# A block of r, k and w with 128 rows instead of 112

## The chip, the cores and the metric

The kernel runs on one core of one Trainium2 chip. The time is that of the device, in microseconds, from one launch; the median of several runs is given. A profile is one further execution, recorded by the hardware profiler; its span runs from the first instruction to the last, and its own time is a little longer.

The names of the engines in the profile: PE is TensorE (PEld its weight loads), DVE is VectorE, ACT is ScalarE, POOL is GpSimd, SP is SyncE, which issues nearly all transfers here.

## The reference

A linear attention with a decaying state (RWKV6) over 4 x 8 heads, 768 steps and 48 columns a head, then a feed-forward block with a hard-swish gate over the 3072 tokens (384 columns, 2048 inside).

```python
for t in range(S):
    kt, vt, rt, wt = (k[:, :, t], v[:, :, t], r[:, :, t], w[:, :, t])
    cur = np.einsum('bhd,bhe->bhde', u[None] * kt, vt)
    y[:, :, t] = np.einsum('bhd,bhde->bhe', rt, state + cur)
    state = wt[:, :, :, None] * state + np.einsum('bhd,bhe->bhde', kt, vt)
...
h = x @ w_in
relu6 = np.clip(h + 3.0, 0.0, 6.0)
g = h * relu6 / 6.0
return (g @ w_out).astype(np.float32)
```

The attention's inputs are 32-bit floats. The weights w_in and w_out come as 64-bit floats, which the kernel converts by itself.

## The kernel before

The sequence is cut into chunks of 128 steps: 4 sequences of 6 chunks, 24 chunks in all (NT). Four chunks make a block of 512 tokens, of which there are 6, and the feed-forward part works block by block. The program for all engines is one list of named steps. Each step has an engine, a function that issues its instructions, and the steps that it must follow; the order of the list is written out by hand in a table (ORDER). Each engine works through its own steps in that order.

For a chunk i, the host lays r, k and w out in DRAM as one block, `feat[i]`. Its rows are the columns of the heads: 48 for the even heads, 16 unused ones, 48 for the odd heads, together GP + D = 64 + 48 = 112. Each row holds 1545 floats, or 6180 bytes: r (512), k (512), and w in 8 pieces of 65 with a final word. On the chip the block lands in a tile `feat_in` of a pool with three buffers. The step feat{i} (load_feat, L343) loads it. The first chunk is loaded in two parts: the columns of w first, and r and k by load_rest (L353). The three buffers also serve the steps refetch{k}, which from about 150 us on read w and the weight words once more, 128 rows of 6144 bytes each, to test their range.

What reads a block, by line:

- L428 (DVE): a scan backwards over w, giving E; L437 (DVE): a scan forwards, giving W
- L448 and L452 (DVE for the first seven chunks, POOL after that): k times E, giving K, and r times W, over W
- L461 (DVE): rk, r times k, for the first nine chunks; PE multiplies it with u (L473) to get the diagonal. For later chunks POOL computes rk from another load, rk_in (L366, then L464)
- PE turns K (L514) and multiplies K with W (L498) for the scores, and so on to the output x of the attention

The weight words come in 16 blocks (step fetch{j}, L391, tile `bits`). ACT makes `more` from them (L400, L405), DVE makes `top` (L411) and adds the two to `w_in` or `w_out` (L415). The feed-forward matmuls stand at L714 and L733 for the first block of tokens, and at L829 and L884 for the others. The latter use sums of weights and inputs that DVE forms beforehand (L776 and the lines after it). L846 and L854 (DVE) and L850 (ACT) belong to the gate, and L902 (DVE) to the output.

In the first 60 us the program has filler matmuls (L1260, on an identity matrix) on PE, put between the steps while the program is built, from a table of assumed times.

SP's queue begins like this (name of the tile, source, rows x elements); bits are the weight words, v_in the values v:

```order
1 L346 DMA feat_in<-in_feat_dram 112x521
2 L354 DMA feat_in<-in_feat_dram 112x1024
3 L349 DMA feat_in<-in_feat_dram 112x1545
4 L361 DMA v_in<-in_tok_dram 128x384
5 L391 DMA bits<-in_moe_w_in_dram 128x3x256
6 L361 DMA v_in<-in_tok_dram 128x384
7 L391 DMA bits<-in_moe_w_in_dram 128x3x256 x2
8 L349 DMA feat_in<-in_feat_dram 112x1545
```

The first two rows are the first chunk's block, the third and the eighth are the next two blocks.

The function general_path holds a second, slower way for inputs out of range. It is behind a branch that these inputs do not take, and the change touches its loads only so that they read the same 112 rows as before.

Of the kernel before, what the change touches and what calls it, by code (L numbers as in the profile page):

```python
# [8 lines left out]
F32 = mybir.dt.float32  # L9
# [12 lines left out]
HL = L // 2  # L22
GP = 64
# [220 lines left out]
def fast_path(tc, feat, tok, wflat, ub, ug, moe_w_in, moe_w_out, out, flag, n_chunks):  # L244
# [3 lines left out]


    nc = tc.nc  # L250
    NT, PR, nf = feat.shape
    HD = tok.shape[3]
    D = PR - GP
    H = HD // D
    P = H // 2
# [11 lines left out]
    with ExitStack() as ctx:  # L267
        const = ctx.enter_context(tc.tile_pool(name="const", bufs=1))
        io = ctx.enter_context(tc.tile_pool(name="io", bufs=3))
# [6 lines left out]
        chunk_of = [(i // NSEQ * 2 + i % 2) * n_chunks + i % NSEQ // 2 for i in range(NT)]  # L276
# [8 lines left out]
        st = [dict() for _ in range(NT)]  # L285
# [52 lines left out]
        n = P * L  # L338
# [2 lines left out]
        plan.ring("rk_in", 2)  # L341

        def load_feat(i):  # L343
            a = io.tile([PR, nf], F32, name="feat_in")
            if i == 0:
                nc.sync.dma_start(out=a[:, 2 * n:], in_=feat[chunk_of[i], :, 2 * n:])  # L346
                nc.scalar.dma_start(out=u_col, in_=ug)
            else:
                nc.sync.dma_start(out=a, in_=feat[chunk_of[i]])  # L349
            st[i].update(a=a, r=a[:, :n].rearrange("q (x t) -> q x t", t=HL),  # L350
                         k=a[:, n:2 * n].rearrange("q (x t) -> q x t", t=HL), w=a[:, 2 * n:])

        def load_rest():  # L353
            nc.sync.dma_start(out=st[0]["a"][:, :2 * n], in_=feat[chunk_of[0], :, :2 * n])  # L354

        def load_u():
            nc.sync.dma_start(out=u_bc, in_=ub.to_broadcast([128, HD]))
# [612 lines left out]
        def when(i):  # L970

            bk, c = divmod(i, BC)
            return BASE[bk] - LAG - (BASE[bk] - BASE[bk - 1]) / BC * (BC - 1 - c) if bk else -99.0
# [20 lines left out]
        for i in range(NT):  # L994
            t = when(i)
            k = START[i] if i < len(START) else when(i - 2) - AHEAD
            first, last = is_first(i), is_last(i)
            dve = i < EARLY
            behind = [f"fetch{BEHIND[i]}"] if i < len(BEHIND) and BEHIND[i] >= 0 else []
            plan.add(f"feat{i}", "SP", 0.45 if i else 1.15, do(load_feat, i), behind + [f"feat{i - 1}"] * (i > 0) + ["later"] * (i == 1), k - 20, kb=735 if i else 294,  # L1000
                     hold=[("feat", [f"K{i}", f"R{i}"] + [f"own{i}"] * (i < BY_PE))])
            plan.add(f"tok{i}", "SP", 0.45, do(load_tok, i), behind + [f"feat{i}"] * (i > 1) + ["later"] * (i < 2), k - 19.9, kb=320,
# [25 lines left out]
            t = k + 1 if i < len(START) else t  # L1028
# [25 lines left out]
            bk, c = divmod(i, BC)  # L1054
# [34 lines left out]

        plan.add("u", "SP", 0.45, load_u, ["fetch3"], -60.0, kb=320)  # L1090
        plan.add("later", "SP", 0.45, load_rest, ["feat0"], key=-999.0, kb=630)

        for j in range(len(pairs)):
            t = CONV[0] + j * CONV[1]
# [12 lines left out]
        for f in range(NFC):  # L1107
            for c0, c1 in parts_of[f]:
                m, x = c1 - c0, c0 // BY_SUM
# [47 lines left out]
        for bk in range(NB):  # L1157
# [7 lines left out]
            for d in range(2 * (bk > 0)):  # L1165
                at = K + U_ / 2 * d
                u, r = f"up{bk}.{d}.", f"read{bk}.{d}."
                name = lambda x: u + str(x) if isinstance(x, int) else r + x
# [41 lines left out]
            for p in range(2 * (bk > 0)):  # L1210
# [4 lines left out]
                d_, r, g_ = f"down{bk}.{p}.", f"out{bk}.{p}.", f"sum{bk}.{p}."  # L1215
# [26 lines left out]
        for k, (which, j) in enumerate(vets):  # L1242
            i = 8 + k // 2
# [23 lines left out]
def general_path(tc, feat, tok, ug, moe_w_in, moe_w_out, out, n_chunks):  # L1267
# [7 lines left out]


    nc = tc.nc
    NT, PR, nf = feat.shape
    HD = tok.shape[3]
    D = PR - GP  # L1280
    H = HD // D
    P = H // 2
# [4 lines left out]
    n2 = 2 * P * L  # L1287

    with ExitStack() as ctx:
        const = ctx.enter_context(tc.tile_pool(name="g_const", bufs=1))  # L1290
        io = ctx.enter_context(tc.tile_pool(name="g_io", bufs=3))
# [4 lines left out]
        st = [dict() for _ in range(NT)]  # L1296

        def load(i):
            a = io.tile([PR, 3, P, L], F32, name="rkw_in")
            b = io.tile([L, H, D], F32, name="v_in", bufs=4)  # L1300
            nc.sync.dma_start(out=a[:, 0:2].rearrange("q c p t -> q (c p t)"), in_=feat[i, :, :n2])
            nc.sync.dma_start(out=a[:, 2].rearrange("q p (a t) -> q (p a) t", a=2),
                              in_=feat[i, :, n2:nf - 1].rearrange("q (x t) -> q x t", x=2 * P)[:, :, 1:])
            nc.sync.dma_start(out=b.rearrange("s h d -> s (h d)"), in_=tok[i, :, 2, :])
            st[i].update(R=a[:, 0], K=a[:, 1], tot=a[:, 2], v=b)

        load(0)
        ub_sb = const.tile([PR, P, 2], F32, name="ub_sb")
        nc.sync.dma_start(out=ub_sb, in_=ug)
        load(1)  # L1310

        w_in = const.tile([128, NFC, NCC, 128], F32, name="w_in_g")
# [24 lines left out]
        for i in range(NA):  # L1337
            a = const.tile([128, 2, P, L], F32, name=f"scores_{i}")
# [147 lines left out]
        for i in range(NT):  # L1486
            if i + 2 < NT:
                load(i + 2)
            own(i)
            for l in range(LEVELS):  # L1490
                score(i, l)
                merge(i, l)
            read(i)
            write(i)
            turn(i)
            if i % GBC == GBC - 1:
                for f in range(NFC):
                    up(i // GBC, f)
                for c in range(GBC):
                    down(i // GBC, c)  # L1500
# [3 lines left out]
def kernel(  # L1504
# [25 lines left out]
    flags = ctx.enter_context(tc.tile_pool(name="flags", bufs=1))  # L1530
    flag = flags.tile([1, 1], I32, name="flag")
    fast_path(tc, feat, tok, wflat, ub, ug, moe_w_in, moe_w_out, out, flag, n_chunks)
    bad = nc.values_load(flag[0:1, 0:1], min_val=0, max_val=128)
    with tc.If(bad > 0):
        general_path(tc, feat, tok, ug, moe_w_in, moe_w_out, out, n_chunks)
# [64 lines left out]
```

## Time and profile before

| | |
|---|---|
| median of 3 runs | 546.07 us (544.54 to 546.16) |
| profiled execution | 545.16 us, span 543.4 us |
| PE busy | 533.5 us, 98% of the span |
| DVE, ACT, POOL busy | 78%, 49%, 20% |
| transfers of queue 1 (SP) | 63.12 MB, 38.0% of the DMA engines' time |
| loads of a block | 24, of 675.9 KB each, median 5.6 us to landing |

A row of the waits reads: engine and step that waited, what ended the wait, then microseconds in total, times, and the longest. A row of the timeline reads: start, length, engine, line, operation, output and inputs, shapes, and in brackets the idle time just before it with what ended it. A row of the transfers gives the number, the size of each and the median time from issue to landing. A row of a stretch gives its length and, for each engine, busy time and instructions, then PE's clock, the mean busy share of the 16 DMA engines, and GB/s.

### The profile page before, as it was taken

The page shows a single profiled execution, that of the slowest core. Times are in us where ns is not written, and L with a number is a line of the kernel's source. Part 1 is how long each engine was busy: PE and PEld are TensorE (multiplying, and loading weights), DVE is VectorE, ACT ScalarE, POOL GpSimd, SP SyncE. Part 2 cuts the span into 40 slices and gives each one's busy share as a digit, 9 for nine tenths or more (in the row PEclk, how much of TensorE's full clock was granted, in tenths as well). Part 3 has the DMA queues.
Part 4 walks back from the last instruction along what each step waited for, and adds up shares of the span by engine and source line. Part 5 has one row for each costly group of instructions (what it writes and reads, how often), then busy time and mean ns, then how long its engine had stood idle before and what let it go on. Part 6 is the DMA issues. An engine that isn't in the chain of part 4 may idle for free.

```text
span 543.4 us, 13407 instructions
## 1 busy us (share of the span) xinstructions
PE 533.5 (98%) x5558; PEld 468.2 (86%) x5558; DVE 423.5 (78%) x726; ACT 267.7 (49%) x657; POOL 111.2 (20%) x111
## 2 busy tenths in 40 slices
PE   8999999999999999999999999999999999999995
PEld 8898876666888999888999888999888999888995
DVE  7898999777899977999978989968889724478531
ACT  3898885333655334546525557425455324264200
POOL 2000002456221126211613154025310000000000
PEclk9999999999999999999999999999999999999999
DMA  8979853434253262655044865032510001000001
GB/s 266 301 192 301 282 178 97 117 111 119 58 144 108 70 179 95 225 190 162 23 146 154 268 212 143 0 106 84 178 58 1 2 16 30 31 0 2 1 29 36
DMA packets 23270, 64.08 MB, mean 118 GB/s; under 512 B 3216, under 2 KB 10544, under 8 KB 23200
## 3 DMA queue, kind: packets, MB, share of 16 engines
q1 hardware_dynamic: 23072, 63.12, 38.0%
q8 instruction: 46, 0.75, 0.6%
q14 instruction: 24, 0.20, 0.1%
q10 hardware_dynamic: 128, 0.00, 0.0%
HBM read 57.31 MB, written 4.72 MB: 114 GB/s over the span
## 4 chain that ended last, share of the span: by engine, by line
PE 93%; DVE 3%; ACT 1%; DMA 1%; issue 1%; POOL 0%; POOLq 0%; DVEq 0%
PE bank L884 28%; PE bank L829 25%; PE bank L714 8%; PE bank L733 8%; PE bankS L884 5%; PE bankS L829 5%; PE y_ps L576 2%; PE y_ps L598 2%; PE bank L498 2%; PE ps L514 2%; PE bankS L1260 2%; PE y_ps L585 2%; DVE g L846 1%; PE ps L473 1%; DMA feat_in<-in_moe_w_out_dram 1%; DVE g L854 1%
## 5 line engine op out<-in xcount | busy, mean ns | idle before, releaser
L850 ACT ACTIVATE clip<-g,three 128x512 f32<-128x512 f32 x80 | 57.0, 722 | 54.1 <-DVE g L846 44.7
L846 DVE TENSOR_TENSOR g<-bank,g 128x512 f32<-128x512 f32 x80 | 53.7, 685 | 10.4 <-PE bank L829 9.2
L854 DVE SCALAR_TENSOR_TENSOR g<-clip,g 128x512 f32<-128x512 f32 x80 | 54.9, 700 | 5.8 <-ACT clip L850 5.8
L884 PE MATMUL bank<-w_out,g 128*128 128x192 f32 x320 | 57.3, 327 | 0.0
L489 ACT ACTIVATE A<-eyes,dg 128x64 f32<-128x64 f32 x192 | 49.5, 338 | 10.9 <-PE y_ps L585 10.6
L884 PEld LDWEIGHTS bank<-w_out,g 128*128 128x128 f32 x320 | 52.8, 190 | 1.2 <-DVE g L854 0.3
L448 POOL TENSOR_TENSOR K<-feat_in,E 112x512 f32<-112x512 f32 x17 | 22.3, 1309 | 133.7 <-DVE W L452 84.8
L714 PE MATMUL bank<-xT,w_in 128*128 128x256 f32 (+1 forms) x216 | 45.6, 362 | 1.2 <-ACT more L405 1.2
L681 ACT COPY xT<-y_ps 48x256 f32<-48x256 f32 x88 | 32.1, 365 | 27.7 <-PE y_ps L585 26.9
L733 PE MATMUL bank<-w_out,g 128*128 128x384 f32 x128 | 43.8, 491 | 0.0
L714 PEld LDWEIGHTS bank<-xT,w_in 128*128 128x128 f32 x216 | 36.5, 190 | 5.8 <-ACT more L405 1.3
L829 PE MATMUL bank<-xT,w_in 128*128 128x256 f32 x160 | 40.4, 380 | 0.1
L844 ACT COPY g<-bank 128x512 f32<-128x512 f32 x50 | 28.8, 582 | 21.2 <-PE bank L829 17.8
L733 PEld LDWEIGHTS bank<-w_out,g 128*128 128x128 f32 x128 | 23.5, 190 | 14.2
L428 DVE TENSOR_TENSOR_SCAN E<-feat_in,back 112x520 f32<-112x520 f32 x24 | 31.4, 1310 | 4.1 <-DMA feat_in<-in_feat_dram 3.1
L900 ACT ACTIVATE o<-bank 128x192 f32<-128x192 f32 x30 | 9.9, 329 | 49.7 <-PE bank L884 49.6
L829 PEld LDWEIGHTS bank<-xT,w_in 128*128 128x128 f32 x160 | 30.1, 190 | 4.5 <-ACT g L844 0.7
L437 DVE TENSOR_TENSOR_SCAN W<-feat_in,start 112x520 f32<-112x520 f32 x24 | 31.4, 1307 | 0.8 <-PE y_ps L576 0.6
L452 POOL TENSOR_TENSOR W<-feat_in,W 112x512 f32<-112x512 f32 x17 | 22.8, 1342 | 44.3 <-DVE W L437 44.3
L829 PE MATMUL bank<-xT,bits 128*128 128x256 f32 x120 | 30.8, 380 | 0.0
L505 DVE COPY_PREDICATED A<-mask,bank 128x256 f32<-128x256 uint8 x48 | 18.6, 441 | 14.9 <-PE bank L498 14.7
L884 PE MATMUL bank<-more,g 128*128 128x192 f32 x160 | 28.7, 328 | 0.0
(290 smaller groups left out, 1135.2 us busy)
## 6 DMA issues: line engine op xcount, KB each, us to landing
feat_in<-in_feat_dram SPq DMA_DIRECT2D x23, 675.9 KB, 5.6
bits<-in_moe_w_in_dram SPq DMA_DIRECT2D x8, 768.0 KB, 10.5
bits<-in_moe_w_out_dram SPq DMA_DIRECT2D x8, 768.0 KB, 5.6
feat_in<-in_moe_w_in_dram SPq DMA_DIRECT2D x8, 768.0 KB, 4.6
feat_in<-in_moe_w_out_dram SPq DMA_DIRECT2D x8, 768.0 KB, 5.0
rk_in<-in_tok_dram SPq DMA_DIRECT2D x15, 384.0 KB, 6.0
v_in<-in_tok_dram SPq DMA_DIRECT2D x24, 192.0 KB, 4.9
out_dram<-o SPq DMA_DIRECT2D x24, 192.0 KB, 2.1
```

The lines of the kernel that those rows point to most:

```text
L428: nc.vector.tensor_tensor_scan(out=E_[:, ::-1], data0=d["w"][:, :0:-1], data1=back.rearrange("q p t -> q (p t)")[:, ::-1], initial=0.0, op ...
L437: nc.vector.tensor_tensor_scan(out=W_, data0=d["w"][:, :-1], data1=starts[i % 2].rearrange("q p t -> q (p t)"), initial=0.0, op0=ALU.mult, ...
L489: nc.scalar.activation(out=d["A"][:, h, :], in_=eyes, func=ACT.Copy, scale=d["dg"][:, h])
L681: nc.scalar.copy(out=blocks[bk]["xT"][g * GP:g * GP + D, :, at:at + HL], in_=st[i]["y_ps"][a][(g ^ a) * GP:(g ^ a) * GP + D, :, :])
L714: nc.tensor.matmul(h_ps[:, :(c1 - c0) * L], lhsT=w_in[:, f // 2, j, f % 2, :], rhs=b["xT"][:, j, c0 * L:c1 * L], start=(j == 0), stop=(j = ...
L733: nc.tensor.matmul(b["o", c][:, :DM], lhsT=g_of(0, f, c), rhs=w_out[:, f, :], start=(f == 0), stop=(f == NFC - 1))
L829: nc.tensor.matmul(b["p", d, c][:, z * HB:(z + 1) * HB], lhsT=weight(W_PLACE[r], d)[:, z, :], rhs=x_at(bk, X_PLACE[r]), start=fresh and z ...
L844: nc.scalar.copy(out=out_, in_=src)
L846: nc.vector.tensor_tensor(out=out_, in0=src, in1=out_of(bk, d, other), op=ALU.add if sign > 0 else ALU.subtract)
L850: nc.scalar.activation(out=c, in_=out_of(bk, d, u), func=ACT.Relu, bias=three, scale=twice)
L854: nc.vector.scalar_tensor_tensor(out=g, in0=blocks[bk]["r", d, u], scalar=6.0, in1=g, op0=ALU.min, op1=ALU.mult)
L884: nc.tensor.matmul(b["d", p, to][:, :h], lhsT=a, rhs=w(), start=(f == 0 and k in (1, 5)), stop=(f == HF - 1 and k in (2, 3, 4)), skip_grou ...
```

## The change

The host adds 16 rows of zeros to each block in DRAM, so it has 128 rows of 6180 bytes. The tile feat_in has 128 rows for these loads too, and a load moves all of them. What the engines read is the view of the first 112 rows, as before.

```diff
-    NT, PR, nf = feat.shape
+    NT, PR, nf = feat.shape[0], ug.shape[0], feat.shape[2]
...
         def load_feat(i):
-            a = io.tile([PR, nf], F32, name="feat_in")
+            b = io.tile([feat.shape[1], nf], F32, name="feat_in")
+            a = b[:PR]
             if i == 0:
-                nc.sync.dma_start(out=a[:, 2 * n:], in_=feat[chunk_of[i], :, 2 * n:])
+                nc.sync.dma_start(out=b[:, 2 * n:], in_=feat[chunk_of[i], :, 2 * n:])
                 nc.scalar.dma_start(out=u_col, in_=ug)
             else:
-                nc.sync.dma_start(out=a, in_=feat[chunk_of[i]])
-            st[i].update(a=a, r=a[:, :n].rearrange("q (x t) -> q x t", t=HL),
+                nc.sync.dma_start(out=b, in_=feat[chunk_of[i]])
+            st[i].update(b=b, r=a[:, :n].rearrange("q (x t) -> q x t", t=HL),
...
         def load_rest():
-            nc.sync.dma_start(out=st[0]["a"][:, :2 * n], in_=feat[chunk_of[0], :, :2 * n])
+            nc.sync.dma_start(out=st[0]["b"][:, :2 * n], in_=feat[chunk_of[0], :, :2 * n])
...
-    laid["feat"] = _np.concatenate([rk.reshape(NT, GP + D, -1), ws.reshape(NT, GP + D, -1), end], axis=2)
+    feat = _np.concatenate([rk.reshape(NT, GP + D, -1), ws.reshape(NT, GP + D, -1), end], axis=2)
+    laid["feat"] = _np.concatenate([feat, _np.zeros((NT, 128 - GP - D, feat.shape[2]), feat.dtype)], axis=1)
```

The same place in SP's queue is now:

```order
1 L347 DMA feat_in<-in_feat_dram 128x521
2 L355 DMA feat_in<-in_feat_dram 128x1024
3 L350 DMA feat_in<-in_feat_dram 128x1545
4 L362 DMA v_in<-in_tok_dram 128x384
5 L392 DMA bits<-in_moe_w_in_dram 128x3x256
6 L362 DMA v_in<-in_tok_dram 128x384
7 L392 DMA bits<-in_moe_w_in_dram 128x3x256 x2
8 L350 DMA feat_in<-in_feat_dram 128x1545
```

Only the number of rows of the loads of a block differs; the lines have moved by one. On every engine the instructions and the semaphores that they wait for stand in the same order as before.

More of the change, by code (lines that the diff above doesn't have):

```diff
@@ L1277, in general_path @@
     nc = tc.nc
-    NT, PR, nf = feat.shape
+    NT, PR, nf = feat.shape[0], ug.shape[0], feat.shape[2]
     HD = tok.shape[3]
@@ L1300, in load @@
             b = io.tile([L, H, D], F32, name="v_in", bufs=4)
-            nc.sync.dma_start(out=a[:, 0:2].rearrange("q c p t -> q (c p t)"), in_=feat[i, :, :n2])
+            nc.sync.dma_start(out=a[:, 0:2].rearrange("q c p t -> q (c p t)"), in_=feat[i, :PR, :n2])
             nc.sync.dma_start(out=a[:, 2].rearrange("q p (a t) -> q (p a) t", a=2),
-                              in_=feat[i, :, n2:nf - 1].rearrange("q (x t) -> q x t", x=2 * P)[:, :, 1:])
+                              in_=feat[i, :PR, n2:nf - 1].rearrange("q (x t) -> q x t", x=2 * P)[:, :, 1:])
             nc.sync.dma_start(out=b.rearrange("s h d -> s (h d)"), in_=tok[i, :, 2, :])
```

## The prediction

> **What bounds the kernel now.** I read the page first: busy shares, the slices and the chain of work that ended last.
>
> ```profile
> PE 533.5 (98%) x5558; PEld 468.2 (86%) x5558; DVE 423.5 (78%) x726; ACT 267.7 (49%) x657; POOL 111.2 (20%) x111
> DMA  8979853434253262655044865032510001000001
> q1 hardware_dynamic: 23072, 63.12, 38.0%
> PE 93%; DVE 3%; ACT 1%; DMA 1%; issue 1%; POOL 0%; POOLq 0%; DVEq 0%
> ```
>
> TensorE (PE) is busy for 533.5 of 543.4 us, and it is 93% of the chain. The DMA engines are busy 38% on average, but nine tenths at the very start. So a change to a transfer can move the end only through a wait of PE. The second view is therefore the list of waits, for PE alone, and then the rows of VectorE (DVE) and SP that name the changed transfer.
>
> ```profile
> PE bankS L1260 <- POOL ident masks.py:199: 1.4, 1, 1.4
> PE bank L714 <- ACT more L405: 1.2, 1, 1.2
> PE bank L829 <- DVE g L846: 0.5, 1, 0.5
> PE bank L829 <- DVE T__3533 L776: 0.2, 1, 0.2
> PE bank L884 <- DVE S__4096 L869: 0.2, 1, 0.2
> DVE E L428 <- DMA feat_in<-in_feat_dram: 3.1, 3, 1.2
> DVE rk L461 <- DMA feat_in<-in_feat_dram: 0.7, 1, 0.7
> ```
>
> No row has PE waiting for a block of r, k and w. What it waits for after its start comes to 1.2 + 0.5 + 0.2 + 0.2 = 2.1 us. DVE waits for a block 3.1 + 0.7 us at four places. The question is whether one of these waits is passed on to PE. The timeline of DVE shows where they lie, and that of PE what comes next:
>
> ```profile
> 3.86 1.25 DVE L428 TENSOR_TENSOR_SCAN E<-feat_in,back 112x520 f32<-112x520 f32 x1 [1.14 <-DMA feat_in<-in_feat_dram]
> 6.54 0.67 DVE L461 TENSOR_TENSOR rk<-feat_in 112x512 f32<-112x512 f32 x1
> 9.64 1.24 DVE L428 TENSOR_TENSOR_SCAN E<-feat_in,back 112x520 f32<-112x520 f32 x1 [1.22 <-DMA feat_in<-in_feat_dram]
> 11.03 0.65 DVE L461 TENSOR_TENSOR rk<-feat_in 112x512 f32<-112x512 f32 x1
> 19.83 0.56 DVE L411 TENSOR_SCALAR top<-bits 128x768 int32<-128x768 int32 x1 [0.62 <-DMA bits<-in_moe_w_in_dram]
> 22.20 0.69 DVE L461 TENSOR_TENSOR rk<-feat_in 112x512 f32<-112x512 f32 x1 [0.68 <-DMA feat_in<-in_feat_dram]
> 48.55 1.24 DVE L428 TENSOR_TENSOR_SCAN E<-feat_in,back 112x520 f32<-112x520 f32 x1 [0.69 <-DMA feat_in<-in_feat_dram]
> 49.94 0.65 DVE L461 TENSOR_TENSOR rk<-feat_in 112x512 f32<-112x512 f32 x1
> ```
> ```profile
> 8.03 0.63 PE L473 MATMUL ps<-u_col,rk 112*64 112x2 f32 x16
> 12.13 0.63 PE L473 MATMUL ps<-u_col,rk 112*64 112x2 f32 x16
> 23.21 1.60 PE L714 MATMUL bank<-xT,w_in 128*128 128x128 f32 x12 [1.18 <-ACT more L405]
> 24.75 0.63 PE L473 MATMUL ps<-u_col,rk 112*64 112x2 f32 x16
> 52.50 0.63 PE L473 MATMUL ps<-u_col,rk 112*64 112x2 f32 x16
> ```
>
> Until 22 us PE never idles because filler matmuls (L1260) stand between its real steps at fixed places. Their number is fixed when the program is built, so an earlier block does not bring the real steps forward; it only widens a margin. The first real wait is the one at 23.21.
>
> **The change, part by part.** Three things: more bytes, another spread over partitions, and 16 more rows written. No instruction is added, removed or moved, and no wait.
>
> *Bytes.* Each of the 24 blocks grows by 16 rows x 6180 B = 98,880 B, in all 2.37 MB: queue 1 goes from 63.12 to 65.49 MB. With one packet per row it gets 24 x 16 = 384 more; the first block is cut into two column parts, so its rows are two packets each, and the sum is 23072 + 400 = 23472.
>
> *The price of one transfer.* Compare a stretch that holds almost only one block of 112 rows with one that holds a load of 128 rows of 6144 B into the same buffer (columns behind the busy times: clock, DMA share, GB/s).
>
> ```profile
> 147.90:150.70 2.80, 2.80 (x15) 2.46 (x14) 2.77 (x6) 0.59 (x1) 0.12 (x1) 1.00 0.99 263
> 185.90:188.70 2.80, 2.80 (x19) 2.80 (x19) 2.77 (x3) 0.63 (x2) 1.48 (x1) 1.00 0.82 281
> ```
>
> First stretch: 2.80 x 0.99 x 16 = 44.4 engine-us for 2.80 x 263 = 736 KB, or 60 engine-us per MB. Second: 2.80 x 0.82 x 16 = 36.7 for 787 KB, or 47 per MB. So the 128-row load uses the engines less although it carries more. A block of 112 rows (0.692 MB) costs 0.692 x 60 / 16 = 2.60 us of every engine. A block of 128 rows (0.791 MB) costs 0.791 x 47 / 16 = 2.32 us if it behaves as the second stretch, and 0.791 x 60 / 16 = 2.97 us if it keeps its present price. The bounds are -0.28 and +0.37 us a transfer. I take the lower, since 128 rows into this buffer is what the second stretch is; the row length, 6180 against 6144 B, stays as the doubt. The times to landing lean the same way:
>
> ```profile
> feat_in<-in_feat_dram SPq DMA_DIRECT2D x23, 675.9 KB, 5.6
> feat_in<-in_moe_w_in_dram SPq DMA_DIRECT2D x8, 768.0 KB, 4.6
> feat_in<-in_moe_w_out_dram SPq DMA_DIRECT2D x8, 768.0 KB, 5.0
> feat_in<-in_wflat_dram SPq DMA_DIRECT2D x6, 768.0 KB, 4.4
> feat_in<-in_feat_dram SPq DMA_DIRECT2D x1, 448.0 KB, 3.9
> feat_in<-in_feat_dram SPq DMA_DIRECT2D x1, 227.9 KB, 3.0
> ```
>
> Over 24 blocks queue 1's share would go from 38.0% to 38.0 - 24 x 0.28 / 543 = 36.8%, or to 39.6% at the other bound.
>
> The Trainium skill (SBUF — State Buffer, section "Door 1: The DMA port swizzle") says that a DMA's bandwidth depends on how many of 16 SBUF ports its partitions reach, each port serving eight fixed partitions, and that all are filled evenly only by 128; by it the transfer takes the lower bound, and the two stretches agree. A rule that speaks against the change stands in DMA: Bandwidth & Descriptors, "How a descriptor splits into AXI transactions": a run that does not start at a multiple of 256 B fetches bytes that it does not use. Rows of 6180 B stay misaligned, so by it the price per row stays and 16 rows more make each transfer a seventh longer, the upper bound. The sum below comes out the same by either, and no run so far separates the two.
>
> *Before 12 us.* The first two blocks, 227.9 + 448.0 + 675.9 KB = 1.38 MB, stand at the head of SP's queue and land one behind the other. With a seventh more they are 1.58 MB: at the present price 0.20 x 60 / 16 = +0.74 us at the end of the second block, at the lower price (1.58 x 47 - 1.38 x 60) / 16 = -0.5 us. Who feels it? The product rk of the first chunk ends at 6.54 + 0.67 = 7.21 and PE takes it at 8.03, so 0.8 us are in hand. That of the second ends at 11.03 + 0.65 = 11.68 and PE takes it at 12.13: 0.45 us in hand, the tightest place. At +0.74, PE and all behind it come 0.3 us later; at -0.5, nothing changes, because the fillers ahead stay. I take 0 and keep +0.3.
>
> *At 23 us.* PE waits here for the third block of weight words, converted by ScalarE (ACT).
>
> ```profile
> 12.81 0.17 ACT L479 COPY dg<-ps 128x8 f32<-128x8 f32 x1 [0.48 <-PE ps L473]
> 21.00 1.07 ACT L400 ACTIVATE more<-bits 128x768 uint16<-128x768 uint32 x1
> 21.95 1.04 ACT L405 ACTIVATE more<-bits 128x768 bf16<-128x768 int32 x1
> ```
>
> ACT has worked without a gap since 12.81 (its rows follow one another; these are the first and the last two of 13), so it, and not the transfer, makes PE wait. DVE began on the same words at 19.83, the moment they landed; ACT came to them at 21.00, so they had 1.2 us in hand. The 0.74 us at most of the blocks ahead of them fit into that. An earlier landing gains nothing, since ACT begins when PE's step at 12.13 lets it. Cost 0.
>
> *At 22.20 and 48.55.* The waits of 0.68 and 0.69 us end in DVE steps whose results PE takes at 24.75 (rk, ended 22.89: 1.9 us in hand) and at 52.50 (rk, which follows E in DVE's order and ended at 50.59). Half a microsecond either way is hidden. Cost 0.
>
> *After 60 us.* DVE waits nowhere for a block there; the DMA share of a slice is mostly 2 to 6 tenths, and blocks are issued well ahead. The 16 extra rows are read by nobody: every use goes through the 112-row view. The tile's bytes per partition are the same, so no other buffer moves. Cost 0, covered by buffers for three blocks.
>
> The sum is 0 us, with bounds of 0 and +0.3 from these steps. The profiled execution took 545.16 us (span 543.4, and 1.8 around it), 0.9 below the median of the three runs, 546.07. I put no change on the median: 546.0 us. The three runs lie 1.62 us (0.30%) apart, and about 0.3%, or 1.6 us, is what a measurement can tell from no change.
>
> **The rivals.**
>
> *The transfers get longer, and nothing else happens.* The pattern of 6180-byte rows keeps the price of 60 engine-us per MB. For it speaks that rows of that length are the only ones with it; against it, that they are also the only full-width loads of 112 rows. Landings get 0.4 us later and the end moves 0 to 0.3 us: 546.1 to 546.4, no change that can be told.
>
> *Slower: the third block of weight words comes after ACT has reached it.* All of PE's real work after 23.21 hangs on it. It decides from +1.2 us of delay on; to lose 1.6 us the words would have to land 1.2 + 1.6 = 2.8 us later. The 0.20 MB ahead of it give 0.74 at the present price, and the third block of r, k and w, issued behind the words, shares engines with them. A price four times as high would be needed for 547.7 us. For it speaks only that the DMA engines are full there (0.94 of them):
>
> ```profile
> 0.00:24.00 24.00, 21.21 (x353) 19.46 (x354) 18.01 (x33) 14.74 (x37) 3.01 (x15) 1.00 0.94 270
> ```
>
> *Faster: POOL's work shifts under DVE's.* A block's transfer is followed in the queue by rk_in, for which POOL waits. When POOL starts, DVE's step beside it stretches:
>
> ```profile
> 152.80 1.00 POOL L464 TENSOR_TENSOR rk<-rk_in 128x384 f32<-128x384 f32 x1 [1.04 <-DMA rk_in<-in_tok_dram]
> 152.84 1.24 DVE L776 SCALAR_TENSOR_TENSOR w_in<-w_in 128x256 f32<-128x256 f32 x1
> 154.12 1.10 DVE L776 SCALAR_TENSOR_TENSOR w_in<-S__1862,w_in 128x256 f32<-128x256 f32 x1
> L776 DVE SCALAR_TENSOR_TENSOR w_in<-w_in,S__1862 x2: 419/422/425, 142.0 to 142.8; 128x256 f32<-128x256 f32 x2
> ```
>
> The two steps lost 1.24 + 1.10 - 2 x 0.42 = 1.5 us, in the one stretch where PE then waits 0.5 us for DVE. If POOL came 0.3 us earlier and missed them wholly, DVE would win 1.5 us and PE at most as much: 544.6 us. But DVE has work on both sides, and a POOL step that moves by 0.3 us meets the neighbour instead; the loss can grow as well as shrink. To pass 1.6 us, a second such place would have to gain too.
>
> **How the numbers follow.** No change with shorter transfers: 0.55. No change with longer ones: 0.28. Faster by over 0.3%, by POOL and DVE falling better, or because the 0.30% between like runs plays into it: 0.10. Slower by over 0.3%, by a late third block or by the same spread: 0.07. The first two together give 0.83 for within 0.3%. The range reaches to the better POOL and DVE case (544.6) and up by the 0.3 us of the second block's step and the spread between like runs: 544.5 to 547.4.
>
> **What would show it.** In the changed kernel's profile: 23472 packets and 65.49 MB on queue 1, with a share near 36.8% (39.6% if the price stays); median landing of the blocks, then 772.5 KB, below 5.6 us (above it in the rival); PE still 98% busy with the same wait of about 1.2 us at L714. I am wrong if PE waits anywhere for a step that waits for a block, if the wait at L714 grows past 2 us, or if the steps of DVE between 147 and 165 us take several microseconds more or less.

## The result, and the profile after

The changed kernel takes 544.55 us (median of 20 runs, 543.9 to 546.21). The kernel before, run beside it, takes 547.25 (20 runs, 544.54 to 556.36). The ratio is 0.9946, with a 95% interval of 0.9927 to 0.9964: half a per cent faster, where I had put my weight on no change. The time itself, 544.55, lies at the lower edge of the range. Two things stand out in these numbers: the median falls by 2.7 us, and the spread of the runs falls from 11.8 to 2.3 us. The ratios of this text leave out runs over 1.5% above the fastest of their kernel, which count as slow; of the 20 before these are 552.72, 554.49 and 556.36, and without them the median before is 546.41 and the spread 5.2 us. In the changed kernel all line numbers are one higher: L714 is now L715.

The profiled execution took 544.22 us, 0.94 less than the one of before. These lines of its page answer to those of before:

```profile
PE 533.3 (98%) x5558; PEld 467.9 (86%) x5558; DVE 425.6 (78%) x726; ACT 267.6 (49%) x657; POOL 113.1 (21%) x111
DMA  8959753333342343745145853032510001000001
q1 hardware_dynamic: 23472, 65.50, 35.4%
q8 instruction: 46, 0.75, 0.6%
PE 92%; DVE 6%; issue 1%; POOL 0%; ACT 0%; DVEq 0%; POOLq 0%
feat_in<-in_feat_dram SPq DMA_DIRECT2D x23, 772.5 KB, 4.4
bits<-in_moe_w_in_dram SPq DMA_DIRECT2D x8, 768.0 KB, 6.2
```

Queue 1 moves 2.37 MB more in less time: 38.0% of 543.4 is 206 us for each engine, 35.4% of 542.5 is 192. A block lands 4.4 us after its issue, where it took 5.6. The waits of PE, and that of DVE for a block:

```profile
PE bankS L1261 <- POOL ident masks.py:199: 1.4, 1, 1.4
PE bank L830 <- DVE g L847: 0.5, 1, 0.5
PE bank L830 <- DVE A L506: 0.2, 1, 0.2
PE bank L830 <- DVE T__3533 L777: 0.2, 1, 0.2
PE bank L885 <- DVE S__4096 L870: 0.2, 1, 0.2
DVE E L429 <- DMA feat_in<-in_feat_dram: 1.7, 2, 1.0
```

The wait of 1.2 us at the first feed-forward matmul is gone from the list. The timeline of PE at that place, and the crowded beginning as one stretch (clock, DMA share and GB/s stand last):

```profile
21.11 0.66 PE L586 MATMUL bank<-A,v_in 64*48 64x64 f32 x32
21.70 1.61 PE L715 MATMUL bank<-xT,w_in 128*128 128x128 f32 x12
23.23 0.63 PE L474 MATMUL ps<-u_col,rk 112*64 112x2 f32 x16
```
```profile
0.00:24.00 24.00, 22.30 (x375) 20.35 (x376) 19.25 (x36) 15.79 (x42) 3.96 (x15) 1.00 0.93 329
```

That matmul starts at 21.70 with no wait; before it started at 23.21 after a wait of 1.18. The DMA engines are as busy as before (0.93 against 0.94), and move 329 GB/s instead of 270. I laid PE's 5558 matmuls of the two profiles side by side. By more than 0.25 us they differ at three places only: the fillers at 6 to 7 us come up to 0.55 us earlier in the changed kernel (the granted clock became full at 5.79 us, not at 6.93), of which 0.27 are left at 21 us; this wait takes the lead to 1.51; and at 330 us 0.5 us are given back. The last matmul ends 1.15 us earlier. The two sums on DVE at 151 us are as slow as before (1.22 and 1.10 us), so the case that I had named for "faster" did not happen.

### The profile page after: what moved, and what is told of

Same layout as the page of the kernel before. It is cut to its first block, busy times and chain, and to the rows that moved or that the text cites. A ratio compares the mean times of both kernels' runs of the same rounds, so it can differ in the third digit from the quotient of the medians.

```text
span 542.5 us, 13407 instructions
## 1 busy us (share of the span) xinstructions
PE 533.3 (98%) x5558; PEld 467.9 (86%) x5558; DVE 425.6 (78%) x726; ACT 267.6 (49%) x657; POOL 113.1 (21%) x111
## 3 DMA queue, kind: packets, MB, share of 16 engines
q1 hardware_dynamic: 23472, 65.50, 35.4%
## 4 chain that ended last, share of the span: by engine, by line
PE 92%; DVE 6%; issue 1%; POOL 0%; ACT 0%; DVEq 0%; POOLq 0%
PE bank L885 29%; PE bank L830 24%; PE bank L715 8%; PE bank L734 8%; PE bankS L885 5%; PE bankS L830 4%; PE y_ps L577 2%; PE bankS L1261 2%; PE ps L515 2%; PE y_ps L599 2%; PE bank L499 2%; PE y_ps L586 2%; DVE g L847 2%; DVE g L855 1%; PE ps L474 1%
## 5 line engine op out<-in xcount | busy, mean ns | idle before, releaser
L855 DVE SCALAR_TENSOR_TENSOR g<-clip,g 128x512 f32<-128x512 f32 x80 | 56.5, 720 | 5.8 <-ACT clip L851 5.8
L715 PE MATMUL bank<-xT,w_in 128*128 128x256 f32 (+1 forms) x216 | 45.5, 362 | 0.0
L715 PEld LDWEIGHTS bank<-xT,w_in 128*128 128x128 f32 x216 | 36.6, 191 | 4.4
```

The costliest lines, as they stand in the source:

```text
L715: nc.tensor.matmul(h_ps[:, :(c1 - c0) * L], lhsT=w_in[:, f // 2, j, f % 2, :], rhs=b["xT"][:, j, c0 * L:c1 * L], start=(j == 0), stop=(j = ...
L855: nc.vector.scalar_tensor_tensor(out=g, in0=blocks[bk]["r", d, u], scalar=6.0, in1=g, op0=ALU.min, op1=ALU.mult)
```

## What made PE wait: the theories

My text had put the wait down to ScalarE, as the list of waits does. The changed kernel speaks against it: the wait went though nothing of ScalarE's work became shorter. In the build, L714 waits for a step of DVE that ended at 21.52 and one of ScalarE that ended at 20.98, both over 1.6 us before 23.21. The step that the row names, a conversion on ScalarE, ended at 22.99; in the changed kernel it ends at 22.68, and the matmul has begun at 21.70, without it:

```profile
21.63 1.05 ACT L406 ACTIVATE more<-bits 128x768 bf16<-128x768 int32 x1
```

**Theory F, the fetch.** PE's own instructions come as 16 KB packets on a queue of their own (q8: 46 packets in the page above, for the 11226 instructions of PE in the trace) through the same DMA engines. The transfers of the kernel before around the second such packet and the same of the changed kernel, each in a stretch of 1.2 to 1.35 us that holds just that packet:

```profile
DMA packets 162, 0.32 MB, mean 239 GB/s; under 512 B 21, under 2 KB 113, under 8 KB 161
q8 instruction: 1, 0.02, 5.8%
```
```profile
DMA packets 178, 0.36 MB, mean 304 GB/s; under 512 B 13, under 2 KB 53, under 8 KB 177
q8 instruction: 1, 0.02, 5.7%
```

The first stretch is 20.50 to 21.85, the second 19.00 to 20.20; the packet records put the packet at 20.54 to 21.80 and at 19.04 to 20.13. Before, PE stands still from 22.04 to 23.21, which is 1.4 us after its packet's end; in the changed kernel it has no wait. Theory F says that PE ran out of instructions. Its rivals say that the data of that matmul (weight words, or their conversion) came late. That q8 serves PE shows in f_wide, below: there PE is 4 to 6 us late in its work, and the first packet starts at 20.13 us, not at 14.12 as before.

**Theory P, POOL under DVE.** When POOL begins with rk_in just before DVE's two sums at L776, these take 1.2 and 1.1 us instead of 0.4 each, and PE loses some 1.3 us. This holds in the kernel before and in the changed one; whether it happens is a matter of half a microsecond.

The letters stand in the expectations below; the rivals of each are named in its text.

## The experiments

Each ratio is against runs of the kernel before beside it, whose medians were 548.05 to 549.55 us. In the lines of the experiments L714 can also be L715, L716 or L718, since some kernels have a few lines more.

**a_again: the kernel before, unchanged.**

> The kernel before, unchanged, once more. It shows how far its runs lie apart and gives a second profile. Theory F (fetch): PE's own instructions come in pieces of 16 KB through the same DMA engines, and in the crowded first 24 us a piece comes late, by an amount that differs from run to run. It expects runs from 544.5 up to several us more, median 546 to 548, ratio 1.000 within 0.3%, and in the profile a wait of PE at the first feed-forward matmul (L714) of 0.5 us or more, directly after a late instruction packet. Theory D (data): the wait at L714 is for a block or for weight words; it expects that wait to end with a landing or a conversion. Theory C (chance): the difference between before and after is one of the chip's runs; it expects a median near 544.6.

Measured: 549.31 us (12 runs, 545.3 to 552.34), ratio 1.0016, interval 0.9981 to 1.0052. Its profile caught a longer run, 548.99 us. The waits of PE up to 60 us, and the stretch just behind the wait; then a stretch of the same length and place in the program of the changed kernel:

```profile
PE bank L714 <- issue: 3.2, 1, 3.2
24.80:31.60 6.80, 6.80 (x45) 6.56 (x43) 4.92 (x9) 3.64 (x16) 0.00 (x0) 0.50 1.06 332
```
```profile
22.00:28.80 6.80, 6.80 (x82) 6.53 (x81) 6.70 (x13) 5.98 (x23) 0.00 (x0) 1.00 1.00 347
```

As F expected, and far from theory C's 544.6, the median is 549.31. The same wait is 3.2 us long here, and the profile now says "issue": PE waited for nothing that it shows. The second instruction packet came at 21.73 to 22.98, and PE went on at 24.50. Behind the wait the granted clock is 0.50 for 6.8 us, in which PE does 45 matmuls where the changed kernel does 82 at full clock. Against the changed kernel, PE is 2.80 us behind at the first feed-forward matmul and 5.95 us behind at 31.7 us. 1.3 us come back at 155 to 165 us, where DVE's sums miss POOL, and 0.5 at 330; the last matmul is 4.3 us late. So one cause costs 1.2 us in one run and some 6 in another. That this makes the spread of all runs of the kernel before is not shown run by run, but the clock fits: in its runs beside the experiments the mean granted clock is 0.996 to 1.000 where the time is under 546 us, and 0.982 to 0.993 where it is 551 to 553.2; the 20 runs of the changed kernel have 0.996 to 1.000.

**e_early and e_late: half of the change each.** The first has 128 rows only in the first three blocks, the second only in the others.

```diff
+            rows = feat.shape[1] if i < 3 else PR     # e_late: PR if i < 3 else feat.shape[1]
...
-                nc.sync.dma_start(out=b, in_=feat[chunk_of[i]])
+                nc.sync.dma_start(out=b[:rows], in_=feat[chunk_of[i], :rows])
```

> Only the first three chunks' blocks (the ones issued in the first 10 us) are loaded with 128 rows; the other 21 with 112. Theory F: all of the gain, ratio 0.993 to 0.997, no wait at the first feed-forward matmul, spread of the runs as small as after's (2 us). Theory D in the form that shorter landings help all along the kernel: a gain of about 3/24 of it, 1.000 within 0.2%.

> The reverse: the first three blocks with 112 rows, the other 21 with 128. Theory F: no gain or little, ratio 0.998 to 1.001, the wait at the first feed-forward matmul still there in the profile, runs spread over several us. The rival (gain all along): 0.994 to 0.996.

Measured: e_early 542.72 us (6 runs, 542.23 to 543.46), ratio 0.9905, interval 0.9868 to 0.9942. e_late 547.5 us (12 runs, 545.37 to 551.96), ratio 0.999, interval 0.9959 to 1.0022. The waits of PE at the first feed-forward matmul, e_early first:

```profile
PE bank L716 <- issue: 0.6, 1, 0.6
```
```profile
PE bank L716 <- ACT more L407: 1.5, 1, 1.5
```

The whole gain sits in the first three blocks; 21 of the 24 bring nothing that can be told. In e_late the blocks lie 128 rows apart in DRAM, as in the changed kernel, so that alone is not what helps. The second instruction packet came at 18.77 in e_early and at 21.04 in e_late. Two of F's numbers for e_early missed: 0.9905 is better than its 0.993 to 0.997, and a wait of 0.56 us is left. e_early is below the changed kernel mainly because its DVE sums at 151 us took 0.41 and 0.42 us (theory P): PE gains 1.3 us on the kernel before between 154 and 163 us, and the changed kernel gains nothing there.

**f_wide and f_wide256: the same work with fewer PE instructions before that matmul.** Both are the kernel before with two fillers of 128 columns made into one, of 512 columns or of 256.

```diff
-            nc.tensor.matmul(still[:, at:at + L], lhsT=ident, rhs=ident, start=n_ == 0, stop=True, skip_group_check=True)
+            if n_ % 2 == 0:
+                nc.tensor.matmul(still[:, at:at + 2 * L].rearrange("q (a j) -> q a j", a=2), lhsT=ident,
+                                 rhs=ident.rearrange("q (a j) -> q a j", a=1).to_broadcast([128, 2, 128]), ...)
```

> The kernel before with 112 rows, but each two filler matmuls of 128 columns are one of 512 columns: about the same time, and some 60 fewer instructions of PE in the first 22 us. Transfers are untouched. Theory F: the piece of instructions that came late is now needed some 60 instructions, or 1 to 3 us, later, so the wait at the first feed-forward matmul falls from 1.2 to under 0.4 us and the ratio is 0.993 to 0.998. Theory D: the wait stays at 1 us or more at that matmul and the time is the same within 0.2%.

> As the kernel with wide fillers, but with 256 columns, so that the fillers take as long as in the kernel before (a filler of 512 columns took four times one of 128, which made PE some 5 us late). Blocks have 112 rows. Theory F: PE comes to the first feed-forward matmul at about 21.7 to 22.3 us and waits there under 0.3 us, since the late piece of instructions is needed some 60 instructions further on, where the wait is under 0.5 us; ratio 0.990 to 0.996. Theory D: the wait of 1 us or more at that matmul stays, 0.999 to 1.001.

Measured: f_wide 551.9 us (11 runs, 551.07 to 553.47), ratio 1.0075, interval 1.005 to 1.01. A matmul of 512 columns for two of 128 made the first group of fillers last 10.8 us instead of 6.7, so all of PE came 5 to 6 us late, and its time tells nothing on F. f_wide256: 545.35 us (12 runs, 543.72 to 555.26), ratio 0.9964, interval 0.9918 to 1.0011, so that the time alone decides nothing. The timeline of PE in f_wide256:

```profile
21.54 1.61 PE L714 MATMUL bank<-xT,w_in 128*128 128x128 f32 x12
25.38 0.92 PE L1261 MATMUL bankS<-ident 128*128 128x256 f32 x3 [1.03 <-issue]
```

This run separates F from the rivals. The weight words arrive as in the kernel before, and the first feed-forward matmul starts at 21.54 without the wait. The wait now stands at 25.38, in front of a filler, which reads only the identity matrix and waits for no semaphore in the trace, so it does not wait for data. Counted in instructions it is the same place: PE stops before its 706th instruction in the trace, after 346 matmuls, 346 weight loads and 13 that only wait or drain, in this kernel and in every other that has this wait. The second packet came at 22.62 to 23.89, and PE went on 1.5 us after its end. F had expected under 0.5 us at the new place; it was 1.03.

**e_pitch: is it the start of the rows?** The kernel before, 112 rows, with rows 6400 bytes apart in DRAM, so that each begins at a multiple of 256 bytes.

```diff
-    laid["feat"] = _np.concatenate([rk.reshape(NT, GP + D, -1), ws.reshape(NT, GP + D, -1), end], axis=2)
+    # as before, and 55 more floats behind each row, which no load reads
```

> The kernel before, 112 rows of 6180 bytes, but in DRAM each row starts at a multiple of 256 bytes (6400 from row to row). If the misaligned start makes the packets long, queue 1's share falls from 38% to below 36% and the time goes the way of the changed kernel, 0.993 to 0.997. If it is the spread of 112 rows over partitions, the share stays at 37.5 to 38.5%, the wait at the first feed-forward matmul stays, and the ratio is 1.000 within 0.25%.

Measured: 549.89 us (12 runs, 545.82 to 554.98), ratio 1.0009, interval 0.9969 to 1.005. The page's row of queue 1, and the first feed-forward matmul:

```profile
q1 hardware_dynamic: 23072, 63.12, 37.6%
24.01 1.82 PE L714 MATMUL bank<-xT,w_in 128*128 128x128 f32 x12 [2.48 <-issue]
```

The share falls by 0.4 points only because this run is longer: 37.6% of its span of 549.9 us is 207 us for each engine, against 206 before. The wait stays. Behind this wait of 2.48 us the clock is 0.50 once more, from 25.3 to 35.5 us. So it is the number of rows, 112 or 128, and not where they begin in DRAM. The Trainium skill (DMA: Bandwidth & Descriptors, "How a descriptor splits into AXI transactions") lets a misaligned run fetch bytes that it does not use; for rows of this length no run here shows a price of it. The other page that the prediction draws on (the Trainium skill, SBUF — State Buffer, "Door 1: The DMA port swizzle") gives each of 16 ports eight fixed partitions. By its table 112 rows reach all 16 ports and leave four of them half filled, so its rule, which counts the ports that are reached, gives no reason for slower rows; the uneven filling might, but the trace does not show the ports.

**f_extra and f_rows: does more to transfer make the packet late?** Both are the changed kernel with a load of 128 rows of 3584 bytes (459 KB) that nobody reads, in f_extra at 4 us behind the second block of weight words, in f_rows between the third and the fourth block of r, k and w.

```diff
+                nc.sync.dma_start(out=extra, in_=wflat[:, :EXTRA])     # EXTRA = 896
```

> The changed kernel with one more load in SP's queue, 128 rows of 3584 bytes, behind the second block of weight words; its data are read by nobody. Blocks keep 128 rows, so their packets stay as short as in the changed kernel. Theory F: the backlog of the DMA engines in the first 20 us grows by 8 x 0.14 = 1.1 us per engine, the third packet of PE's instructions ends 0.7 to 1.5 us later than the 20.1 of the changed kernel, and PE waits 0.7 to 1.6 us at the first feed-forward matmul, 1.4 to 1.6 us after that packet's end; time 545 to 547. Theory D: the load is behind the words and blocks that PE needs first, so the wait stays under 0.3 us and the time at 544.2 to 545.

> The changed kernel (128 rows), with one transfer more that nobody reads: 128 rows of 3584 bytes, 459 KB, on SP's queue between the third and the fourth block of r, k and w (f_extra had the same load at 4 us, behind the second block of weight words, which moved the second instruction packet by 0.4 us only). Theory F: the extra rows stand in the engines between 14 and 19 us, just when the packet is asked for; the 6180-byte rows end some 1.0 to 1.4 us later (459 KB at 330 to 400 GB/s), the packet starts at 20.0 to 20.4 us instead of 19.04, and PE stops at instruction 706 until 22.5 to 22.9, a wait of 0.7 to 1.3 us where the changed kernel has none; 545 to 546.5. Rival (only rows that are long in time, 355 ns, hold the packet up): the packet moves by under 0.5 us and there is no wait; 544.3 to 545.

Measured: f_extra 544.7 us (10 runs, 544.26 to 545.92), ratio 0.995, interval 0.9913 to 0.9987; no wait, packet at 19.45 (the text above calls it the third; it is the second of the span). f_rows 545.07 us (10 runs, nine of 544.0 to 545.8 and one of 687.18), ratio 0.9929, interval 0.989 to 0.9968. The wait of PE in f_rows:

```profile
PE bank L718 <- issue: 0.2, 1, 0.2
```

F as I had put it, with the packet behind all that is queued, missed both times: the packet of f_rows started at 18.97, not at 20.0 or later. 459 KB more in the engines held it up little or not at all (counted from the start of the first packet, it came 0.7 us later than in the changed kernel: 5.81 us against 5.07). What F's rival in the text of f_rows says, that only transfers which take long do so, is nearer to what was measured.

**f_defer: does one block fewer before the packet help?** The kernel before, with the fourth block's load put behind two blocks of weight words on SP's queue.

```diff
+        names.insert(names.index("u"), names.pop(names.index("feat3")))
```

> The kernel before (112 rows), with one transfer put elsewhere on SP's queue: the fourth block of r, k and w (issued at 9.60 us) goes out behind the fourth and fifth block of weight words instead, at about 20 us. Nothing changes on PE, DVE, ACT or POOL. Theory F (the second 16 KB packet of PE's own instructions can't get through while rows of 6180 bytes fill the engines; they fill them from 14.5 to 21 us before): with one block instead of two in that time, its rows end by about 18 us, the packet starts by 19.5 us at the latest, PE passes instruction 706, the first feed-forward matmul, by 21.9 us, and the wait of 1.18 us is gone (runs of before: 1.2 to 3.2). Time 544 to 546 if chunk 3 is not late by it (its first reader on DVE stands at 27.4 us), later by up to 3 us if it is. Rival (the conversions of the weight words make PE wait there): the third block of words is queued ahead of both blocks and lands as before, so the wait of 1.2 to 3.2 us stays at that matmul.

Measured: 550.97 us (12 runs, 548.24 to 552.83), ratio 1.0028, interval 0.9994 to 1.0062. The waits of PE up to 40 us, and the stretch behind the longest:

```profile
PE ps L475 <- DVE rk L463: 3.0, 3, 2.0
PE bank L716 <- ACT more L407: 1.4, 1, 1.4
32.60:38.60 6.00, 6.00 (x32) 5.80 (x31) 3.92 (x9) 3.69 (x14) 0.00 (x0) 0.50 0.26 67
```

F's number missed here too: the packet came at 21.27, and the wait stayed at 1.4 us (the profile names ScalarE for it again, as it did for the kernel before and e_late). The load that was put off came late for chunk 3, which cost PE another wait of 2.0 us, and the clock fell to 0.50 behind that one. Why did it not help? With the 112 rows of the third block alone beside them, the packets of the values v (1536 bytes) still took 119 ns each between 14 and 21 us, against 65 in the changed kernel.

**e_not13: theory P by itself.** The changed kernel with 112 rows in the block of chunk 13 alone, whose transfer lies ahead of the load that POOL waits for at 150 us.

```diff
+            rows = PR if i == 13 else feat.shape[1]
```

> The changed kernel, but the block of chunk 13 (issued at about 145 us) is loaded with 112 rows. In the changed kernel rk_in, queued behind this block, lands 1.1 us earlier than in the kernel with three early blocks, POOL starts at 150.66, and two DVE steps (L776) take 1.22 and 1.10 us in place of 0.41 and 0.42. Theory P (POOL under DVE): with 112 rows for this one block POOL starts after those DVE steps have begun, they take 0.42 us each, and PE gains 1.0 to 1.5 us between 150 and 165 us; time 542.5 to 543.6, ratio 0.989 to 0.993. The rival, that the late blocks cost time in many places, expects 543.9 to 544.8, no different from the changed kernel.

Measured: 543.05 us (12 runs, 542.4 to 543.87), ratio 0.9906, interval 0.9869 to 0.9942. The timeline of POOL and DVE, in the changed kernel and then in e_not13:

```profile
150.66 1.52 POOL L465 TENSOR_TENSOR rk<-rk_in 128x384 f32<-128x384 f32 x1 [0.49 <-DMA rk_in<-in_tok_dram]
151.24 1.22 DVE L777 SCALAR_TENSOR_TENSOR w_in<-w_in 128x256 f32<-128x256 f32 x1
152.50 1.10 DVE L777 SCALAR_TENSOR_TENSOR w_in<-S__1862,w_in 128x256 f32<-128x256 f32 x1
```
```profile
150.72 0.41 DVE L778 SCALAR_TENSOR_TENSOR w_in<-w_in 128x256 f32<-128x256 f32 x1
151.16 0.43 DVE L778 SCALAR_TENSOR_TENSOR w_in<-S__1862,w_in 128x256 f32<-128x256 f32 x1
151.20 1.25 POOL L466 TENSOR_TENSOR rk<-rk_in 128x384 f32<-128x384 f32 x1 [1.56 <-DMA rk_in<-in_tok_dram]
```

With POOL's data half a microsecond later, the first sum is through and the second has begun before POOL begins, and both are short, as theory P had it. Against the changed kernel PE gains 1.3 us between 154 and 162 us (it was 0.53 us ahead there and is 1.81 ahead behind it); the median is 1.5 us lower.

**best_wide and best_four: which version beats both.** best_wide is e_early with the fillers of f_wide256. best_four has 128 rows in the first four blocks (`if i < 4`) and 112 in the rest. The second is also the last test of what held the packet up.

> 128 rows for the first three blocks only (the best so far, 542.72) and each pair of fillers made into one of 256 columns, as in f_wide256. Theory F: PE reaches instruction 706 only at about 24 us, as in f_wide256 (due at 24.35 there), and with 128 rows the second packet should start by 20 to 21.5 us, so it is in time: the 0.56 us that e_early waits at its first feed-forward matmul go, 542.0 to 542.5. If PE's clock is granted later with wider fillers, or the packet is asked for later by as much as PE gets later there, no gain: 542.7 or a little over.

> 128 rows for the first four blocks (e_early has three), 112 for the rest. Theory F, as it stands after f_defer and f_rows: the second instruction packet comes late where the packets beside it take long (rows of 6180 bytes between 14 and 21 us: 372 to 421 ns in the kernels with 112 rows there, 342 in e_early, 241 in the changed kernel), and not where there is only more of them. With the fourth block at 128 rows too, the rows take about 241 ns between 14 and 21 us, the packet starts within 1.5 us of e_early's 18.77 or earlier, and the 0.56 us that e_early still waits at its first feed-forward matmul fall to 0 to 0.2: 542.0 to 542.6, if GpSimd's work beside the two sums on DVE at 151 us falls as in e_early; 543.4 to 544.2 if it falls as in the changed kernel (1.22 and 1.10 us for the two instead of 0.41 and 0.42). Rival (the number of rows in the early blocks makes no difference to the packet, e_early only had an early clock): the rows still take over 320 ns, or the wait stays at 0.5 us or more.

Measured: best_wide 543.54 us (6 runs, 542.15 to 544.01), ratio 0.9892, interval 0.9839 to 0.9945; no wait at the 706th instruction, as F had it, but no gain on e_early in the median, and above the 542.0 to 542.5 expected. best_four 542.98 us (6 runs, 542.24 to 543.78), ratio 0.9903, interval 0.9865 to 0.9941; its profiled execution took 542.24; expected were 542.0 to 542.6. The stretch from 14 to 21 us (DMA share and GB/s stand last) of before, of the changed kernel, and of best_four, here with its waits of PE up to 60 us and the two sums on DVE:

```profile
14.00:21.00 7.00, 6.91 (x159) 6.21 (x159) 5.31 (x13) 6.92 (x17) 0.00 (x0) 1.00 1.05 274
```
```profile
14.00:21.00 7.00, 6.82 (x158) 5.85 (x156) 5.26 (x12) 6.71 (x16) 0.00 (x0) 1.00 1.01 381
```
```profile
14.00:21.00 7.00, 6.82 (x187) 5.97 (x185) 5.42 (x12) 6.92 (x14) 0.00 (x0) 1.00 1.01 378
PE bankS L1262 <- POOL ident masks.py:199: 1.4, 1, 1.4
PE ps L475 <- DVE rk L463: 0.2, 1, 0.2
150.66 0.41 DVE L778 SCALAR_TENSOR_TENSOR w_in<-w_in 128x256 f32<-128x256 f32 x1
151.11 0.42 DVE L778 SCALAR_TENSOR_TENSOR w_in<-S__1862,w_in 128x256 f32<-128x256 f32 x1
```

With the fourth block's 16 rows more, e_early's last 0.6 us of wait are gone, as F had it: PE reaches the place at the same time (21.16 and 21.13 us), and the packet ends at 19.09 instead of 20.12. PE's lead over e_early is 0.60 us behind 21 us, of which 0.2 us are left at the end. e_early, e_not13, best_four and best_wide cannot be told apart in time; each is some 0.95 to 1.1% below the kernel before, and 1 to 2 us below the changed one, which was not run beside them.

All profiles together, from their packet records: the mean time of a 6180-byte row that began between 14 and 21 us, the start of the second instruction packet, and the wait of PE before its 706th instruction.

| kernel | a row, ns | packet starts, us | wait, us |
|---|---|---|---|
| before | 388 | 20.54 | 1.18 |
| a_again | 412 | 21.73 | 3.16 |
| e_pitch | 417 | 21.35 | 2.48 |
| f_defer | 421 | 21.27 | 1.36 |
| e_late | 364 | 21.04 | 1.54 |
| e_early | 342 | 18.77 | 0.56 |
| f_rows | 241 | 18.97 | 0.16 |
| f_extra | 241 | 19.45 | 0 |
| the changed kernel | 242 | 19.04 | 0 |
| e_not13 | 241 | 17.82 | 0 |
| best_four | 241 | 18.02 | 0 |

The kernels with wider fillers reach the place later and are left out. Where rows take 241 ns, PE waits 0.2 us at most; where they take 342, 0.6; above that, 1.2 to 3.2. The wait also depends on when PE comes to the place, and that moves with the start of the full clock, at 4.4 to 7.2 us in these profiles. So e_early's 0.56 us do not come from slow rows alone: its packet ended at 20.12 us and the changed kernel's at 20.13, but PE was there at 21.13 and 21.77. In both the matmul started 1.57 us after that end, so the packet of the changed kernel came only just in time.

## Why the prediction was wrong

*At 23 us: this step failed.* "ACT has worked without a gap since 12.81 [...] so it, and not the transfer, makes PE wait", and then "Cost 0". PE waited for its own instructions, and the third block of weight words was not what it needed there. I took the name in the list of waits as the cause, although the step of ScalarE that ended at 22.99 is not one that L714 waits for, and the two steps that it does wait for had ended by 21.52; the row names the last event on ScalarE's semaphore before PE went on, though PE needed only an earlier one, and in a_again, where the wait was 3.2 us, the same row reads "issue". The term that I set at 0 was worth 1.18 us in the profiled pair. It is worth more in the median, since the waits of 2.48 us and over also took the clock down; with a_again's wait of 3.16 us PE was 5.95 us late at 31.7 us. That the time still fell into the range is luck: its lower end stood for the case of POOL and DVE, which did not come.

*The price of one transfer: right.* The lower bound was the right one. The 6180-byte rows, those of 23 blocks, took 57.2 us of each engine before and 51.2 after, 0.26 us less for each block; forecast was 0.28. Queue 1's share fell further than my 36.8%, to 35.4%, because other transfers that run beside the blocks got shorter too: the rows of 3072 bytes took 39.9 us of each engine before and 32.7 after. Packets and bytes came out as written (23472; 65.50 MB against 65.49).

*Before 12 us, at 22.20 and at 48.55: right.* Fillers hold the real steps in place; PE does not move there by more than the clock's start. DVE's waits for a block fell from 3.8 to 1.7 us, and PE gained nothing by them.

*After 60 us: right for the changed kernel, by luck.* PE's lead of 1.5 us stays within half a microsecond up to the end. But e_not13 shows that a shift of half a microsecond in one transfer is worth 1.3 us at 151 us. I had that case as a rival, with the right place and price (1.5 us); it did not come with this change.

*The spread.* I counted the 0.30% between three runs as noise of measurement. Most of it very likely had a cause inside the kernel, the length of this wait, and the change took it away: the spread of the runs fell with the wait, and in every profile where it was 2.48 us or more the clock fell behind it.

## What to carry to other kernels

A wait on TensorE that the profile puts down to an engine which had long been done, or to "issue", may be a wait for instructions: look at the instruction queue among the transfers, count the instructions to the wait, and see whether it stays at the same count when the work is cut otherwise. Where such a packet has to pass through crowded DMA engines, the time that each neighbouring packet takes can count more than the number of bytes, as it did here, and loads over all 128 rows can be quicker than smaller ones over 112. A kernel whose runs scatter by 2% may have one early wait that sometimes grows long enough to cost TensorE its clock.

## What the runs showed of the hardware

- Instruction packets stand among the DMA queues, and come late beside slow data (the second at 20.5 to 21.7 us beside blocks of 112 rows, at 17.8 to 19.5 beside blocks of 128). PE runs on for a while without the packet, and stops until 1.3 to 1.6 us after its end. The Trainium skill (Runtime: NRT & Kernel Launch, "Instruction fetch mechanics") describes the refill in blocks of 16 KiB, 256 instructions, by a queue of the sequencer's own, and calls its cost mostly hidden; the packets agree (46 of 16 KB), but in the kernel before the cost is 1.2 to 3.2 us, once.
- After waits of PE of 1.98 us (f_defer), 2.48 (e_pitch) and 3.16 (a_again) the granted clock was 0.50 for 6.8 us (10.2 in e_pitch); after 1.54 us or less it stayed at 1.00. The Trainium skill (TensorE: Matmul & The Clock Gate, "What's actually happening") lets the clock fall after an idle window of about 3.4 us; here less was enough.
- A block of 112 rows of 6180 bytes uses the DMA engines longer than one of 128 rows (2.49 against 2.22 us of each engine), and what runs beside it is slower: 274 against 381 GB/s between 14 and 21 us, at full DMA share in both. Why is open: the start of the rows in DRAM is excluded by e_pitch, and no run here shows how the rows spread over ports.
- Open too is in what order a DMA engine takes an instruction packet among the rows of other queues, so why the packet waits for long rows but hardly for more of them.
